# Transposing the attention probabilities in two halves of 64 rows, each into a PSUM bank of its own

## The chip, the cores and the metric

One core of a Trainium2 chip runs the whole program. The metric is device time in microseconds (us), as a median of several runs. Five engines work side by side, each through its own list of instructions: PE (TensorE, matmuls; its weight loads are listed apart as PEld), DVE (VectorE), ACT (ScalarE), POOL (GpSimd) and SP (SyncE, which issues most transfers). They wait for each other by semaphores.

## The reference, cut to what matters

```
# attention: B, H, S, D = 8, 8, 576, 64, a causal window of 64 positions
scores = scale * np.matmul(q, k.transpose(0, 1, 3, 2))
mask = (rel >= 0) & (rel < window)            # rel = query position - key position
scores = np.where(mask, scores, -1000000000.0)
attn = np.exp(scores - scores.max(-1))        # divided by its sum + 1e-9
attn_out = np.matmul(attn, v)
# x = attn_out as 4608 tokens of 512 = 8 heads x 64
# experts: a token with x @ w_skip > 0 goes to the best of 8 experts by x @ w_gate
# out = x + gate_w * (relu(x @ w1[e]) @ w2[e]) for those tokens, out = x for the others
```

## The kernel before, in words

**Tiles.** The 4608 tokens are worked off in 36 tiles `t` of 128 queries: two blocks of 64 queries (`hf` = 0 and 1), all 8 heads. By its window a block of queries sees its own 64 keys and the 64 before them, so the scores of a tile are 128 queries x 8 heads x 128 keys.

**The steps of one tile.** `score(t)` (L238, L252): the mask (`band`) and then the products of q and k go into the PSUM tile `ps`, two banks, on quarters of PE's array (64 rows x 64 columns each). `soften(t)`: DVE takes the maximum (L271) and subtracts it (L272), ACT makes the exponential (L277); the result `s` lies in SBUF with the 128 queries on the partitions. `transpose_p(t)` (L279 to L287): PE turns `s` head by head, so that the keys lie on the partitions, into `pt` in PSUM, and ACT copies that to `ptm` in SBUF (L286). `tile_out(t)` with `av_tile` (L388): PE multiplies `ptm` by the values (and by ones for the sums, and by columns for the router) into `av`; DVE reads it from L399 on and divides by the sums. A transpose on PE loads the data as weights and streams an identity matrix through them.

**The gate.** In most tiles a piece of the router's projection of v goes through PE as well: `pw` (L336) or its transpose `pk` (L344). ACT copies both out of PSUM. `pt`, `pw` and `pk` share one pair of PSUM banks (tag "t", bufs=2) in turn.

**The order.** It is written out by hand. Iteration t issues `score(t + 1)`, the gates, `soften(t)`, `tile_out(t - 2)`, `transpose_p(t - 1)`, and between these the loads, the stores and the routing of finished groups of 6 or 8 tiles: counts on PE (L517, L520), lists of tokens on POOL and PE (L560). Each engine keeps to its order. So PE goes scores, gate, `av`, transposes, and ACT goes gate copy, exponential, copies of `pt`.

After the attention part comes the expert part, whose work starts from the routed lists; its matmuls keep PE busy to nearly the end. The short transposes `px` (L895) that the prediction reads belong to it: token rows turned before an expert's first product, some with only 32 rows.

Of the kernel before, what the change touches and what calls it, by code (L numbers as in the profile page):

```python
# [8 lines left out]
F32 = mybir.dt.float32  # L9
# [11 lines left out]
P = 128  # L21
# [123 lines left out]
def window_attention_moe(ctx: ExitStack, tc, a, out):  # L145
    nc = tc.nc
# [6 lines left out]
    psum = ctx.enter_context(tc.tile_pool(name="psum", bufs=1, space=PSUM))  # L153
# [9 lines left out]
    ident = const.tile([P, P], F32, name="ident")  # L163
# [115 lines left out]
    def transpose_p(t):  # L279
        s = ss.pop(t)  # L280
        ptm = ptp.tile([P, 8, P], F32, name="ptm")
        for r in range(2):
            pt = psum.tile([P, 4, P], F32, name="pt", tag="t", bufs=2)
            for p in range(4):
                nc.tensor.transpose(pt[:, p], s[:, 4 * r + p], ident)  # L285
            nc.scalar.copy(ptm[:, 4 * r : 4 * r + 4], pt)  # L286
        pts[t] = ptm  # L287

    ss, pts, vs = {}, {}, {}
# [847 lines left out]
    with tc.manual_schedule():  # L1137
# [42 lines left out]
        for t in range(NT - 1):  # L1180
            m, r = divmod(t, 9)
# [18 lines left out]
            if t >= 1:  # L1200
                transpose_p(t - 1)
# [22 lines left out]
        drip()  # L1224
        routes(1)
        transpose_p(NT - 2)
        raise_e(NT - 1)
        routes(1)
        drip()
        tile_out(NT - 2, psc.tile([P, 2, 4, P], F32, name="ps").rearrange("p a b c -> p a (b c)"))  # L1230
        drip()
        routes(1)
        transpose_p(NT - 1)
        pxs = [psc.tile([P, 2, 4, P], F32, name="ps"), pav.tile([P, 2, 512], F32, name="av")]
        pxs = [pxs[0][:, 0].rearrange("p a b -> p (a b)"), pxs[1][:, 0]]
# [173 lines left out]
    with tc.If(more > 0):  # L1409
        with tc.For_i(0, more, 1) as i:  # L1410
# [15 lines left out]
            for qi in range(NQ):  # L1426
                both = []
# [58 lines left out]
```

## Time and profile before

| | |
|---|---|
| time, median of 3 runs | 415.93 us (414.9 to 416.22) |
| the profiled execution's own time | 417.13 us |
| its span in the profile | 415.4 us |
| granted TensorE clock, mean | 0.995 |
| transposes in the attention part | 288, on record with 282 ns each |
| copies of them on ACT | 72, 581 ns each |

The span is the profiled execution from its first to its last instruction; its time is a little longer. Instructions on PE overlap, so that the time on record of one is longer than the distance to the next: what a stage costs is read from its piece in the chain.

### The profile page before, as it was taken

To read this page: it belongs to the slowest core of one execution; us is meant where nothing else is said; L and a number is where in the kernel's file an instruction comes from. 1 tells how busy PE (TensorE), PEld (TensorE's weight loads), DVE (VectorE), ACT (ScalarE), POOL (GpSimd) and SP (SyncE) were. 2 spreads that over 40 slices of the span, in tenths; PEclk is the share of its full clock that TensorE was granted. 3 is DMA by queue.
4 is the path that set the end of the run, shared out by engine and by line. 5 is a ranking of instruction groups with operands and counts; after the bars stand their busy time and mean duration, and the time that the engine had idled before them with its cause. 6 is when DMAs were issued, how large, how long until landed. Compare 5 with 4: busy or idle time off the path is not lost.

```text
span 415.4 us, 11519 instructions
## 1 busy us (share of the span) xinstructions
PE 392.6 (95%) x4623; PEld 327.6 (79%) x4623; DVE 301.7 (73%) x547; ACT 216.7 (52%) x373; POOL 159.6 (38%) x296
## 2 busy tenths in 40 slices
PE   8898999999999898989999999999999999999794
PEld 3576787877878677879988798898898889988673
DVE  3586899899799795999468789565455486658871
ACT  2675877767677694536224445244335345533450
POOL 1521268567958878477204114022024030100110
PEclk9999999999999998999999999999999999999999
DMA  8999999999995694866605777645136886741510
GB/s 279 408 336 386 405 361 377 411 395 300 394 412 186 212 358 145 234 230 194 224 0 175 255 271 216 225 170 174 55 134 208 266 259 211 245 157 52 184 48 21
DMA packets 35096, 99.41 MB, mean 239 GB/s; under 512 B 4480, under 2 KB 5888, under 8 KB 35040
## 3 DMA queue, kind: packets, MB, share of 16 engines
q1 hardware_dynamic: 30560, 87.22, 60.1%
q0 software_dynamic: 3200, 9.58, 6.5%
q10 hardware_dynamic: 1280, 1.85, 1.2%
q8 instruction: 37, 0.61, 0.6%
q14 instruction: 19, 0.16, 0.1%
HBM read 84.57 MB, written 14.39 MB: 238 GB/s over the span
## 4 chain that ended last, share of the span: by engine, by line
PE 64%; issue 13%; DMA 10%; DVE 4%; POOL 4%; ACT 3%; POOLq 0%; ACTq 0%; SPq 0%; another core or an unknown queue 0%; DVEq 0%
PE av L388 8%; PE pt L285 7%; PE p L918 6%; PE ps L252 5%; PE p L919 5%; PE p L920 5%; DMA out<-yo,les 5%; PE yv L918 3%; PE yv L919 3%; PE yv L920 3%; PE ps L238 2%; PE pw L336 2%; PE yw L919 2%; PE yw L918 2%; PE yw L920 2%
## 5 line engine op out<-in xcount | busy, mean ns | idle before, releaser
L852 DVE TENSOR_TENSOR wlo<-raw,whi 128x1024 fp32r<-128x1024 f32 x70 | 86.3, 1244 | 15.9 <-ACT whi L848 14.2
L1022 POOL DMA_INDIRECT out<-yo,les x18 | 17.6, 976 | 147.7 <-DVE yo L1013 138.0
L982 ACT ACTIVATE hh<-p 128x256 fp32r<-128x256 f32 (+4 forms) x56 | 22.9, 410 | 98.3 <-PE p L920 84.5
L848 ACT CAST whi<-raw 128x1024 fp32r<-128x1024 f32 x72 | 74.2, 1046 | 0.0
L918 PE MATMUL p<-xp,whi 128*128 128x256 f32 (+4 forms) x192 | 58.2, 303 | 0.4 <-ACT xp L896 0.4
L919 PE MATMUL p<-xp,whi 128*128 128x256 f32 (+4 forms) x192 | 57.1, 297 | 0.2 <-DVE xp L899 0.2
L920 PE MATMUL p<-xp,wlo 128*128 128x256 f32 (+4 forms) x192 | 56.8, 296 | 0.0
L985 DVE SCALAR_TENSOR_TENSOR hl<-p,hh 128x256 fp32r<-128x256 f32 (+4 forms) x56 | 25.2, 451 | 43.5 <-ACT hh L982 28.0
L277 ACT ACTIVATE s<-s 128x1024 f32<-128x1024 f32 x36 | 38.1, 1059 | 31.8 <-DVE s L272 31.7
L271 DVE TENSOR_REDUCE mx<-ps 128x8 f32<-128x1024 f32 x36 | 43.6, 1211 | 6.7 <-PE ps L252 6.7
L272 DVE TENSOR_TENSOR s<-ps,mx 128x1024 f32<-128x1024 f32 x36 | 44.1, 1225 | 4.6
L388 PEld LDWEIGHTS av<-vm,ptm 128*64 128x64 f32 x992 | 34.7, 136 | 13.3 <-issue 6.2
L388 PE MATMUL av<-vm,ptm 128*64 128x74 f32 x992 | 39.8, 230 | 4.2 <-issue 1.7
L286 ACT COPY ptm<-pt 128x512 f32<-128x512 f32 x72 | 38.2, 581 | 8.2 <-PE pt L285 8.0
L285 PE MATMUL pt<-ident,s 128*128 128x128 f32 x288 | 39.9, 282 | 0.0
L918 PEld LDWEIGHTS p<-xp,whi 128*128 128x128 f32 x192 | 36.2, 188 | 3.0 <-ACT xp L896 0.7
L919 PEld LDWEIGHTS p<-xp,whi 128*128 128x128 f32 x192 | 36.2, 188 | 1.2 <-DVE xp L899 0.5
L920 PEld LDWEIGHTS p<-xp,wlo 128*128 128x128 f32 x192 | 36.1, 188 | 0.0
L252 PE MATMUL ps<-k,q 64*64 64x128 f32 x1024 | 33.6, 270 | 1.5 <-DMA q<-qT 1.5
L285 PEld LDWEIGHTS pt<-ident,s 128*128 128x128 f32 x288 | 31.6, 143 | 2.5 <-issue 0.3
L252 PEld LDWEIGHTS ps<-k,q 64*64 64x64 f32 x1024 | 30.0, 133 | 4.3 <-issue 2.3
L357 POOL COPY vm<-vm 64x1184 f32<-64x1184 f32 x16 | 18.6, 1166 | 31.9 <-ACT vm L356 26.7
(243 smaller groups left out, 819.4 us busy)
## 6 DMA issues: line engine op xcount, KB each, us to landing
raw<-wq SPq DMA_DIRECT2D x72, 512.0 KB
vm<-vp SPq DMA_DIRECT2D x15, 592.0 KB
vT<-vT SPq DMA_DIRECT2D x16, 512.0 KB
out<-x SPq DMA_DIRECT2D x32, 256.0 KB
q<-qT SPq DMA_DIRECT2D x14, 512.0 KB
k<-kT SPq DMA_DIRECT2D x7, 640.0 KB
k<-kT SPq DMA_DIRECT2D x7, 512.0 KB
kt<-kT SPq DMA_DIRECT2D x8, 256.0 KB
```

The lines of the kernel that those rows point to most:

```text
L252: nc.tensor.matmul(ps[64 * hf : 64 * hf + 64, r, p], q[h, p], k[h, :, p], start=False, stop=p == 3, skip_group_check=True,)
L271: nc.vector.tensor_reduce(mx, flat, axis=AX.X, op=ALU.max)
L272: pace[0] = nc.vector.tensor_tensor(s, flat, mx.unsqueeze(2).to_broadcast([P, 8, P]), op=ALU.subtract)
L277: nc.scalar.activation(s, s, AF.Exp, scale=0.125)
L285: nc.tensor.transpose(pt[:, p], s[:, 4 * r + p], ident)
L286: nc.scalar.copy(ptm[:, 4 * r : 4 * r + 4], pt)
L388: nc.tensor.matmul(av[64 * hf : 64 * hf + 64, h // 4, (h % 4) * VW : (h % 4 + 1) * VW], ptm[:, (h % 2) * 4 + h // 2, 64 * hf : 64 * hf + 6 ...
L848: nc.scalar.copy(ring[n % RING][0], raw_of[n])
L852: by.tensor_tensor(lo, raw_of[n], hi.bitcast(F32), op=ALU.subtract)
L918: nc.tensor.matmul(o, lh, rh, start=first, stop=False, skip_group_check=parts)
L919: nc.tensor.matmul(o, lh, rl, start=False, stop=False, skip_group_check=parts)
L920: nc.tensor.matmul(o, ll, rh, start=False, stop=last, skip_group_check=parts)
```

## The change

`transpose_p` splits the 128 queries of a tile into the halves 0 to 63 and 64 to 127. Each half has one PSUM bank that holds its 64 queries for all 8 heads; before, each bank held all 128 queries for 4 heads. The sixteen transposes alternate between the halves, and each reads 64 partitions of `s` and the matching 64x64 corner of the identity. The two copies come after all of them, and each writes eight runs of 64 columns into `ptm`, where the layout is as before.

```
-        for r in range(2):
-            pt = psum.tile([P, 4, P], F32, name="pt", tag="t", bufs=2)
-            for p in range(4):
-                nc.tensor.transpose(pt[:, p], s[:, 4 * r + p], ident)
-            nc.scalar.copy(ptm[:, 4 * r : 4 * r + 4], pt)
+        both = [psum.tile([P, 8, 64], F32, name="pt", tag="t", bufs=2) for _ in range(2)]
+        halves = [slice(64 * hf, 64 * hf + 64) for hf in range(2)]
+        for h in range(8):
+            for pt, q in zip(both, halves):
+                nc.tensor.transpose(pt[:, h], s[q, h], ident[q, q])
+        for pt, q in zip(both, halves):
+            nc.scalar.copy(ptm[:, :, q], pt)
```

On PE, a tile in the middle of the attention part, from the gate to the next tile's mask, before the change (`pt_916` and `pt_922` are the two banks; "waits" names the engine whose semaphore is waited for; x13 means 13 such rows):

```order
L336 MATMUL pw_875<-vT_701,wg_77 32x256 x3
L388 MATMUL av_888<-vm_312,ptm_835 64x74 [waits DVE_49]
L388 MATMUL av_888<-vm_312,ptm_835 64x74
L388 MATMUL av_888<-vm_312,ptm_835 64x74 [waits Activation_49]
L388 MATMUL av_888<-vm_312,ptm_835 64x74 x13
L285 MATMUL pt_916<-ident_74,s_806 128x128 [waits PE_49]
L285 MATMUL pt_916<-ident_74,s_806 128x128 x3
L285 MATMUL pt_922<-ident_74,s_806 128x128 [waits Activation_49]
L285 MATMUL pt_922<-ident_74,s_806 128x128 x3
L238 LDWEIGHTS identb_75
```

The same place of such a tile with the change (two lines further down in the program; the pattern of the last two rows of transposes goes on to sixteen):

```order
L338 MATMUL pw_774<-vT_571,wg_77 32x256 x3
L390 MATMUL av_787<-vm_210,ptm_727 64x74 [waits DVE_49]
L390 MATMUL av_787<-vm_210,ptm_727 64x74 [waits Activation_49]
L390 MATMUL av_787<-vm_210,ptm_727 64x74 x14
L286 MATMUL pt_811<-ident_74,s_698 128x64 [waits PE_49]
L286 MATMUL pt_812<-ident_74,s_698 128x64 [waits Activation_49]
L286 MATMUL pt_811<-ident_74,s_698 128x64
L286 MATMUL pt_812<-ident_74,s_698 128x64
```

The wait for ACT, which frees the second bank, has moved from the fifth transpose to the second, and in `av` the wait for the second copy from the third matmul to the second. On ACT, the gate's copy, the exponential and the copies of `pt` in one tile before the change:

```order
L338 COPY vw_731<-pw 128x256 [waits PE_49]
L277 ACTIVATE s<-s 128x1024 [waits DVE_49]
L286 COPY ptm<-pt 128x512 [waits PE_49] x2
L364 COPY vm<-vm 64x592
L377 COPY vt<-vm 64x592
```

and with it:

```order
L340 COPY vw_779<-pw 128x256 [waits PE_49]
L277 ACTIVATE s<-s 128x1024 [waits DVE_49]
L288 COPY ptm<-pt 128x8x64 [waits PE_49] x2
L366 COPY vm<-vm 64x592
L379 COPY vt<-vm 64x592
```

Nothing changes place here; the two copies have another target shape.

## Rows read from the trace of the kernel before

**Rows 1.** The page: busy us (share of the span) xinstructions of each engine.

```profile
PE 392.6 (95%) x4623; PEld 327.6 (79%) x4623; DVE 301.7 (73%) x547; ACT 216.7 (52%) x373; POOL 159.6 (38%) x296
```

**Rows 2.** Busy time of each engine in a stretch, PE's clock, DMA share, GB/s.

```profile
core 0: us, PE busy (x) PEld busy (x) DVE busy (x) ACT busy (x) POOL busy (x), PEclk, DMA share, GB/s
34.99:90.67 55.68, 55.63 (x1165) 44.73 (x1161) 50.52 (x94) 41.34 (x74) 29.34 (x59) 1.00 1.03 392
```

**Rows 3.** The chain that ended last, 36 to 48 us: start, us, what.

```profile
37.67 1.02 PE pt L285 x8
38.70 0.34 PE ps L238 x4
39.03 0.87 PE ps L252 x32
39.91 0.57 PE pw L336 x8
40.48 1.18 PE av L388 x32
...
43.90 0.37 PE pk L344 x2
```

**Rows 4.** The same chain, 78 to 95 us.

```profile
77.99 0.22 PE pt L285 x2
```

**Rows 5.** DVE in order of time: start, us, instruction [idle before <-releaser].

```profile
34.99 1.22 DVE L271 TENSOR_REDUCE mx<-ps 128x8 f32<-128x1024 f32 x1
...
41.71 0.17 DVE L399 TENSOR_SCALAR r<-av 128x8 f32<-128x8 f32 x1 [0.23 <-PE av L388]
...
90.67 1.21 DVE L271 TENSOR_REDUCE mx<-ps 128x8 f32<-128x1024 f32 x1
...
124.24 1.21 DVE L271 TENSOR_REDUCE mx<-ps 128x8 f32<-128x1024 f32 x1
...
127.90 1.21 DVE L271 TENSOR_REDUCE mx<-ps 128x8 f32<-128x1024 f32 x1
```

**Rows 6.** DVE's waits from 24 to 95 us: total us, times, longest.

```profile
DVE r L399 <- PE av L388: 4.2, 6, 3.1
DVE r L399 <- PE av L560: 0.7, 1, 0.7
DVE r L399 <- PE av L520: 0.6, 2, 0.4
```

**Rows 7.** Weight loads in order of time: four short transposes; scores after a stall.

```profile
287.29 0.32 PEld L895 LDWEIGHTS px<-ident,xg 32*128 32x128 f32 x4 [0.20 <-issue]
...
16.31 0.13 PEld L252 LDWEIGHTS ps<-k,q 64*64 64x64 f32 x1 [1.36 <-issue]
...
16.31 0.18 PEld L252 LDWEIGHTS ps<-k,q 64*64 64x64 f32 x4 [1.36 <-issue]
```

**Rows 8.** ACT, one tile in order of time; then its groups by shape.

```profile
37.60 1.06 ACT L277 ACTIVATE s<-s 128x1024 f32<-128x1024 f32 x1 [0.42 <-DVE s L272]
38.69 1.07 ACT L286 COPY ptm<-pt 128x512 f32<-128x512 f32 x2
...
L286 ACT COPY ptm<-pt 128x512 f32<-128x512 f32 x72 | 38.2, 581 | 8.2 <-PE pt L285 8.0
L356 ACT COPY vm<-pk 128x144 f32<-128x144 f32 x16 | 4.5, 284 | 5.1 <-PE pk L344 3.4 <-POOL lh L468 0.8 <-DMA vm<-vp 0.6
```

**Rows 9.** In order of time: waits between DVE, POOL and PE after 95 us.

```profile
95.10 0.30 POOL L537 TENSOR_TENSOR gds<-gds,gohb 128x64 f32<-128x64 f32 x1 [2.01 <-DVE gds L530]
...
112.41 0.20 DVE L482 TENSOR_REDUCE gmx<-lg 128x6 f32<-128x48 f32 x1 [1.94 <-POOL lg L469]
...
138.44 1.25 PE L388 MATMUL av<-vm,ptm 128*64 128x74 f32 x32 [1.43 <-POOL vm L357]
```

**Rows 10.** ACT in order of time: a copy that waits for PE.

```profile
140.69 0.58 ACT L286 COPY ptm<-pt 128x512 f32<-128x512 f32 x1 [1.59 <-PE pt L285]
```

**Rows 11.** The waits over the whole span: the scores for q.

```profile
PE ps L252 <- DMA q<-qT: 1.5, 2, 1.1
```

## The prediction

> **What bounds the kernel now.** Read the busy shares first [rows 1]: TensorE (PE) 95%, VectorE (DVE) 73%. That is an average over an attention part (36 tiles, to about 165 us) and an expert part; the change touches the first alone. So the next view is the chain that ended last, in order of time [rows 3]: from 36 to 48 us, as in most of 34 to 113 us, nothing but PE stands in it, piece after piece. One tile is band 0.34, scores 0.87, a gate piece (`pw` 0.57 in some tiles, `pk` 0.37 in others), `av` 1.18 and the transposes `pt` 1.02. With `pw` that is 3.98 us, with `pk` 3.78.
>
> A chain shows what ended last and not how close the next engine is, so DVE comes next. Where DVE waits for nobody, it starts a tile's maximum 3.66 us after the one before (124.24 to 127.90 [rows 5]). Between 34.99 and 90.67 us it starts 14 further tiles in 55.68 us, 3.98 each. It waits at L399, the first instruction that reads `av` [rows 5, 6]. DVE is therefore only 0.1 to 0.3 us a tile behind PE, and this small number, not the 1.02 us of the transposes, is what the change can win.
>
> DMA is as full as it gets in this stretch (share 1.03, 392 GB/s [rows 2]), but the scores wait for a load of q only twice in the whole span, 1.5 us in all [rows 11].
>
> **What the change costs and saves on PE.** Eight transposes of 128x128 become sixteen of 64x128 into 128x64, in pairs that use rows 0 to 63 and 64 to 127 of the array. Each streams 64 columns in place of 128 and loads as many weight columns as before, 128.
>
> Streaming: in the chain two old transposes take 0.22 us [rows 4], so 0.11 us for 128 columns. The scores are recorded as 32 matmuls of 128 columns on quarter tiles, and take 0.87 us [rows 3]: 0.109 for each four. Four tiles in the time of one means that tiles which share columns and differ in rows stream side by side. So a new pair streams in about 0.055 us.
>
> Loading: the four `px` transposes at 287.29 us have 32 rows, 128 weight columns and short matmuls, all in one row group; the four loads take 0.32 us; with one taken as long as the scores' load below, 0.13, that is (0.32 - 0.13)/3 = 0.063 us from load to load [rows 7]. That is the floor within one row group. Do the two groups load side by side? When the scores start after a stall, one load lasts 0.13 us on record and all four together 0.18 [rows 7]: the fourth begins 0.05 after the first, not the 0.18 that three loads of 0.06 in a row would make. The four tiles differ in rows and in columns, so this speaks for overlap between row groups without isolating it.
>
> So a pair costs between 0.06 (loads side by side) and 0.12 (in series). I take 0.0625, nearest to the rows that hold both facts. The old stage is 8 x 0.109 = 0.87 plus 0.15 around it = 1.02. The new one is 8 x 0.0625 = 0.50 plus 0.15 = 0.65. **Saved: 0.37 us of PE a tile**, 5.2 over the 14 tiles above.
>
> The same load, by the Trainium skill ("TensorE: Matmul & The Clock Gate", section "LDWEIGHTS (loading the stationary operand)"), takes columns/1.2 ns whatever the rows, which is about 107 ns for 128 columns, an estimate from that page. By that rule the pair would be bound by its load and the stage would stay at 1.0 us. The `px` row of this trace shows 0.06 us, so the measurement decides for the smaller price; the rule makes one of the rivals.
>
> **ScalarE (ACT).** Each copy moves 512 elements a row as before; only the target is now eight runs of 64. The copy of 512 takes 581 ns, and one of 144 elements in runs of nine 284 [rows 8], so short runs cost nothing that shows: I take 0, at most 0.05 each. The copies now wait for all sixteen transposes, where the first waited for four. In a steady tile this is hidden: the copies of 38.69 us stand in ACT's order behind the exponential of 37.60 to 38.66 [rows 8]; the transposes of that tile stand in the chain from 37.67 [rows 3], and the shorter stage would be done by 38.3. Without that cover (ACT waits for PE, as at 140.69 [rows 10]) the first copy starts at the eighth pair, not the fourth transpose: 0.50 against 0.44, plus the start of a stage, 0.1 us later. There are some five such tiles; I count -0.3 us.
>
> The second transpose now needs the second bank at once, half a stage earlier. Queued behind it on PE is the next tile's score, which DVE reads a whole tile later. The bank's reader is the gate's copy, which ACT makes before the exponential, so I count nothing; if it came late it would cost up to 0.4 in that tile.
>
> **What of it reaches the end.** In 34.99 to 90.67 PE's 55.63 us busy [rows 2] would need 50.4, less than DVE's 14 x 3.66 = 51.2. DVE becomes the bound, and what is won is what DVE waited. From below: the waits listed for 24 to 95 us are 4.2 + 0.7 + 0.6 = 5.5, less the one of 3.1, a single stall that I take to have another cause, so 2.4; shorter waits aren't listed [rows 6]. From above: 55.68 - 51.2 = 4.4, too much, as DVE has routing work of its own in these tiles. I take 3.5, a little over the middle, since a wait of under 0.2 stands in nearly every tile.
>
> After 95 us little more is won. GpSimd (POOL) starts a stretch at 95.10, released by DVE, and works through it until DVE waits 1.94 for it at 112.41; at 138.44 PE waits 1.43 for it again [rows 9]. These are shifted with DVE's 95 us, and a tile won between is lost there. The expert part follows attention and shifts as a whole.
>
> Sum: -3.5 + 0.3 = **-3.2 us**. The profiled execution took 417.13 us (span 415.4), 1.2 above the median of 415.93, so 413.9 beside it and **412.7** as a median. A difference under 0.3% (1.25 us) can't be told from none.
>
> **Rivals.**
> 1. *The pairs load in series* (the other side). Place: the transposes. 16 x 0.0625 + 0.15 = 1.15 us, 0.13 more than now. In the 14 or so tiles before 95 us in which DVE waits, that is 1.8 us, and PE's tiles after 112 us (3.78 and 3.98 against DVE's 3.66) lose a few tenths more: +2.0, 417.9 us. It decides from a pair of 0.109 us upward. For it: no row has two loads that differ in rows alone. Against: four loads within 0.05 us.
> 2. *A load costs what its columns cost at half the rate*, 0.107 us, in both groups at once. The stage stays at 1.0 and the time at 416. Against it the `px` row; for it only that full transposes at 0.11 would hide such a load.
> 3. *PE gets faster and something else takes the wait.* After DVE's subtraction come the exponential, the copies, then the gate, `av` and L399. In the tile of 37.60 us [rows 3, 8] the first copy ends at 38.69 + 0.54 = 39.23; 0.15 for a change of stage, 0.57 of gate, 1.18 of `av` and the 0.05 from its end to L399 make 41.2, against DVE free at 41.71 - 0.23 = 41.5 [rows 5]. There are only 0.3 us of room: if the copies slip by that, or the DMA at 392 GB/s can't deliver faster, less than 1.25 us is left: about 415.3.
>
> **Chances.** The forecast 0.64, rival 1 0.14, rival 2 0.10, rival 3 0.12. So faster 0.64, same 0.22, slower 0.14. The range: the upper bound of DVE's waits, 4.4 + 0.5 for the tiles from 24 us, and 1 us for a shorter chain in the last tiles make about -6, 409.9. Upward it takes in rivals 2 and 3 and reaches toward rival 1: 417.0. The forecast's own range is 410 to 414.6.
>
> **What would show it.** The transposes' piece of the chain at about 0.65 us and a new pair every 0.06; the loads 16 to a tile. DVE's starts 3.66 to 3.75 apart between 35 and 91 us, with L399's waits nearly gone; POOL's wait at 112 still there, slightly longer. ACT's copies still at 0.58. Wrong at the first step if the stage is 1.0 or more; wrong at the second if it is 0.65 and DVE's starts stay at 3.9 with the wait for ACT or a load in the chain.

## The result and the profile after

The changed kernel takes 420.01 us (median of 4 runs, 419.56 to 421.99) beside 416.0 of the old one on the same chip: 1.0108 times, with a 95% interval of 1.0082 to 1.0134. **It is slower by 4.0 us; forecast was 3.2 faster.** The profiled execution took 419.56 us, with a span of 417.7.

The first part of the change did what was forecast. The page's rows for the engines and for the copies (busy, mean ns of one | idle before):

```profile
PE 387.5 (93%) x4911; PEld 323.2 (77%) x4911; DVE 302.2 (72%) x547; ACT 217.4 (52%) x373; POOL 158.9 (38%) x296
...
L288 ACT COPY ptm<-pt 128x512 f32<-128x512 f32 x72 | 38.3, 583 | 8.7 <-PE pt L286 8.5
```

The copies last 583 ns, as before, and PE is busy 5 us less [rows 1]. The chain that ended last, as in [rows 3], shows the shorter stage and what came with it:

```profile
40.30 1.19 PE av L390 x32
41.48 0.64 PE pt L286 x16
42.13 0.34 PE ps L238 x4
42.47 0.65 PE ps L252 x21
43.12 0.94 issue
44.05 0.65 PE ps L252 x11
44.70 0.37 PE pk L346 x2
```

The stage takes 0.64 us (forecast 0.65). But in the middle of the scores, after 21 of 32 matmuls, PE stands still for 0.94 us and waits for nothing that the profile shows ("issue"). The same stretch of DVE's tiles as in [rows 2], now 13 tiles in place of 14:

```profile
core 0: us, PE busy (x) PEld busy (x) DVE busy (x) ACT busy (x) POOL busy (x), PEclk, DMA share, GB/s
34.60:90.70 56.10, 49.90 (x1195) 39.36 (x1191) 46.71 (x86) 39.87 (x70) 26.72 (x53) 1.00 1.02 386
```

A tile takes 56.10 / 13 = 4.32 us, where it took 3.98. At 34.60 the changed kernel was 0.4 us ahead; at its last maximum (156.66 us in place of 152.90) it is 3.8 behind, which is the loss. PE's waits from 24 to 95 us (total, times, longest), where the old kernel had one "issue" wait, of 1.7 us:

```profile
PE av L390 <- issue: 3.1, 4, 1.5
PE ps L252 <- issue: 2.0, 2, 1.0
PE pt L286 <- issue: 1.1, 2, 0.9
PE pw L338 <- issue: 0.6, 1, 0.6
PE pw L338 <- DMA vT<-vT: 0.5, 1, 0.5
```

Nine waits of 6.8 us name no one ("issue"), and 0.5 us is a wait for a load. They strike the scores, `av`, the transposes and the gate alike, so it is not one instruction's fault. PE in order of time shows their rhythm:

```profile
44.05 0.65 PE L252 MATMUL ps<-k,q 64*64 64x128 f32 x11 [0.94 <-issue]
44.63 0.44 PE L346 MATMUL pk<-ident,vw 128*128 128x128 f32 x2
45.00 1.26 PE L390 MATMUL av<-vm,ptm 128*64 128x74 f32 x32
46.19 0.71 PE L286 MATMUL pt<-ident,s 64*128 64x64 f32 x16
46.83 0.41 PE L238 MATMUL ps<-band,identb 64*64 64x512 bf16 x4
47.07 1.04 PE L252 MATMUL ps<-k,q 64*64 64x128 f32 x32
48.04 0.64 PE L338 MATMUL pw<-vT,wg 128*32 128x256 f32 x8
48.61 0.99 PE L390 MATMUL av<-vm,ptm 128*64 128x74 f32 x22
50.07 0.60 PE L390 MATMUL av<-vm,ptm 128*64 128x74 f32 x10 [0.47 <-issue]
...
54.89 0.60 PE L252 MATMUL ps<-k,q 64*64 64x128 f32 x11
56.53 0.88 PE L252 MATMUL ps<-k,q 64*64 64x128 f32 x21 [1.04 <-issue]
...
61.32 0.60 PE L390 MATMUL av<-vm,ptm 128*64 128x74 f32 x11
63.45 0.87 PE L390 MATMUL av<-vm,ptm 128*64 128x74 f32 x21 [1.53 <-issue]
```

From 44.05 to the next stall stand 11 + 2 + 32 + 16 + 4 + 32 + 8 + 22 = 127 matmuls, in the next stretch 127 again, then 126. (An fp32 matmul of the program is recorded as two passes, so sixteen for the scores are 32.) Each has its weight load, so a stall comes every 254 instructions or so. With PE's few semaphore instructions counted as well, in the order in which the records start, it is 256 to the instruction: eight of the nine stalls stand at record 193 or at 193 plus a multiple of 256. The ninth (0.5 us at 27.41) does not, and its cause stays open. What comes in such pieces is on the page, in the rows of queue 8 (packets, MB, share); first the changed kernel:

```profile
q8 instruction: 39, 0.64, 0.6%
```

and the old one:

```profile
q8 instruction: 37, 0.61, 0.6%
```

9822 PE instructions (4911 matmuls and as many loads) in 39 packets are 252 a packet; in the old kernel 9246 in 37 are 250, and a packet is 16 KB. With the semaphore instructions PE has 9945 records and 9359, and in every kernel of this case the number of packets in queue 8 is the number of PE's records divided by 256, rounded up. So PE's own instructions come through the DMA queues in blocks of 256. The single records of the trace give both ends, in us from the span's start (every 256th PE instruction counted from one stall, beside the packets of queue 8):

```
kernel   a block begun   packet of the next starts, ends   next block begun   stall
after         44.05             47.68   48.57                  50.07           0.47
after         50.07             54.12   55.02                  56.53           1.04
after         56.53             60.73   62.04                  63.45           1.53
before        52.35             55.03   56.03                  58.66           none
before        58.66             61.04   62.05                  64.30           none
after        136.35            136.64  137.79                 144.00           none
```

In these rows of the changed kernel PE goes on 1.4 to 1.5 us after the packet's end (1.2 in the shortest of the eight stalls): that is the step from landing to execution. The packet starts 3.6 to 4.2 us after the block before it was begun where DMA is full, and 0.3 us after at 136 us, where it isn't. Together a block that ends in a stall takes about 6 us, and PE gets no more than 256 instructions in that time. The old kernel was close to it: 1165 matmuls and their loads in 55.68 us [rows 2] are 9.1 blocks, 6.12 us each, and its packets mostly ended 2.2 to 2.6 us before they were needed, about 1 us earlier than the 1.2 to 1.5 that PE needs. The changed kernel has 2 x 1195 / 13 = 184 instructions a tile in place of 2 x 1165 / 14 = 166. At the 6.01 us that its own blocks took in this stretch they make its 4.32 us a tile. That is a sum and no test, as both come from the same stretch; the tests are the kernels below with other counts.

The 3.6 to 4.2 us are not a fixed price of full queues. Between 33 and 95 us, at the same DMA share of 1.03, the old kernel's packets started 1.8 to 3.1 us after the block before was begun, and in the changed kernel blocks without a stall had theirs after 2.8 to 3.0 us and took 5.2 to 5.5 (begun at 69.49, 80.71 and 86.23). Why they started sooner is not shown.

### The profile page after: what moved, and what is told of

The parts are those of the page before. It is cut to its first block, busy times and chain, and to the rows that moved or that the text cites. A ratio compares the mean times of both kernels' runs of the same rounds, so it can differ in the third digit from the quotient of the medians.

```text
span 417.7 us, 12105 instructions
## 1 busy us (share of the span) xinstructions
PE 387.5 (93%) x4911; PEld 323.2 (77%) x4911; DVE 302.2 (72%) x547; ACT 217.4 (52%) x373; POOL 158.9 (38%) x296
## 4 chain that ended last, share of the span: by engine, by line
PE 42%; issue 21%; DMA 12%; DVE 12%; POOL 8%; ACT 3%; POOLq 0%; ACTq 0%; SPq 0%; DVEq 0%
PE av L390 6%; DMA out<-yo,les 5%; PE p L920 4%; PE p L921 4%; PE p L922 4%; PE ps L252 3%; DVE s L272 3%; PE pt L286 2%; DVE mx L271 2%; DMA q<-qT 2%; PE yv L920 2%; PE yv L921 2%; PE yv L922 2%; DVE x L403 2%; DMA raw<-wq 2%
## 5 line engine op out<-in xcount | busy, mean ns | idle before, releaser
L854 DVE TENSOR_TENSOR wlo<-raw,whi 128x1024 fp32r<-128x1024 f32 x70 | 85.0, 1226 | 15.8 <-ACT whi L850 15.6
L390 PEld LDWEIGHTS av<-vm,ptm 128*64 128x64 f32 x992 | 36.6, 139 | 16.7 <-issue 8.4
L390 PE MATMUL av<-vm,ptm 128*64 128x74 f32 x992 | 42.3, 234 | 7.2 <-issue 3.2
L252 PE MATMUL ps<-k,q 64*64 64x128 f32 x1024 | 35.2, 270 | 4.5 <-DMA q<-qT 2.4
L286 PE MATMUL pt<-ident,s 64*128 64x64 f32 x576 | 26.5, 231 | 1.1 <-issue 1.1
L734 POOL DMA_INDIRECT xg<-out,les x18 | 24.5, 1363 | 6.1 <-issue 4.6
```

Source lines behind the costliest of these rows:

```text
L252: nc.tensor.matmul(ps[64 * hf : 64 * hf + 64, r, p], q[h, p], k[h, :, p], start=False, stop=p == 3, skip_group_check=True,)
L286: nc.tensor.transpose(pt[:, h], s[q, h], ident[q, q])
L390: nc.tensor.matmul(av[64 * hf : 64 * hf + 64, h // 4, (h % 4) * VW : (h % 4 + 1) * VW], ptm[:, (h % 2) * 4 + h // 2, 64 * hf : 64 * hf + 6 ...
L854: by.tensor_tensor(lo, raw_of[n], hi.bitcast(F32), op=ALU.subtract)
```

## Experiments

Theory **F**: PE waits for blocks of its own instructions. Rivals: **D**, the loads of q, k and v can't come faster; **C**, the later copies; **P**, PE's own time decides; **G**, a block takes 6 us whatever else the queues carry; **H**, loads in pieces come late themselves. Behind each time stands its ratio to the old kernel on the same chip, with the 95% interval.

**1. Order of the halves, copies alone.** `half_by_half` keeps sixteen transposes but runs one half after the other; `late_copies` keeps the eight old transposes and copies after all of them.

```
half_by_half:  for pt, q in zip(both, halves):
                   for h in range(8):
                       nc.tensor.transpose(pt[:, h], s[q, h], ident[q, q])
late_copies:   for r, pt in enumerate(both): (four transposes of 128 rows)
               for r, pt in enumerate(both): nc.scalar.copy(...)
```

> The sixteen transposes in another order: all eight of one half of the queries, then all eight of the other, so that no two neighbours use different rows. As many PE instructions as the changed kernel, but a stage as long as the old one or longer. Theory F (PE waits for its own instructions, which come in blocks of 256 through the full DMA queues): the stage goes back to 1.0 to 1.2 us, the number of instructions decides all the same, the stalls without a named cause stay about 127 matmuls apart between 37 and 91 us, DVE's tiles stay at 4.2 to 4.4 us, 419 to 423 us. Rival D (the loads of q, k and v can't come faster than 373 GB/s): PE asks for them as slowly as before, so 416 to 418 us. Rival C (the copies that start after all sixteen): as D, 416 to 418, by the longer stage alone.

Measured 421.53 us, 1.0133 (1.0097 to 1.0168). The chain of `half_by_half`:

```profile
48.03 0.95 PE pt L286 x16
48.98 0.34 PE ps L238 x4
49.32 0.87 PE ps L252 x32
50.20 0.57 PE pw L338 x8
50.77 0.92 PE av L390 x22
51.68 0.15 issue
```

The stage is 0.95 us, still 0.07 less than the old 1.02, and yet the kernel is 1.3 per cent slower: neither PE's time nor a faster demand for loads can do that. Its 13 tiles from 36.23 to 93.47 us have the same 1195 matmuls, 4.40 us a tile, and nine of its ten unnamed stalls up to 100 us stand at record 193 plus a multiple of 256 again. F holds; D, C and P miss their times here.

> The old kernel with its eight transposes of 128 rows, but with both copies after all eight: the one part of the change that puts the copies later, with neither halves nor more instructions. Theory F: 416 to 416.5 us, tiles of 3.98 us between 35 and 91 us. Rival C: 418 or more, with ACT's copies in the chain.

Measured 416.48 us, 1.0014 (0.9991 to 1.0036): the copies cost next to nothing. C falls again.

**2. More instructions, at little PE time.** `pad_after` adds to the changed kernel eight matmuls of one column a tile, ahead of `av`:

```
for i in range(8):
    nc.tensor.matmul(av[64 * (i % 2) : 64 * (i % 2) + 64, 0, 4 * VW + i : 4 * VW + i + 1],
                     onesb[:, 0:64], onesb[:, 0:1], start=True, stop=True, ...)
```

> The changed kernel with eight more small matmuls a tile ahead of av (one column each, written where nobody reads): 16 more PE instructions a tile, as many as the change itself added, and little PE time, 0.1 to 0.25 us beside the 0.37 that the change took away. Theory F: the number of instructions decides: a tile of about 199 records at 256 in 6.0 us takes 4.6 to 4.7 us, 14 tiles 4 to 5 us more than in the changed kernel, 424 to 428 us, with stalls still 126 or 127 matmuls apart. Rival P (PE's own time decides): a tile stays shorter than the old one, 421 us or less.

Measured 426.8 us, 1.0292 (1.024 to 1.0343). In order of time the eight push `av` back by 0.15 us where nothing stalls:

```profile
52.00 0.29 PE L389 MATMUL av<-onesb 128*64 128x1 bf16 x8
52.15 1.23 PE L395 MATMUL av<-vm,ptm 128*64 128x74 f32 x32
```

The tiles from the seventh maximum to the twentieth, busy time and counts:

```profile
36.68:95.18 58.50, 51.18 (x1301) 40.70 (x1296) 46.95 (x87) 39.82 (x70) 26.65 (x53) 1.00 0.98 359
```

So PE's tile (3.61 with `pw` in the forecast, plus 0.15) is shorter than the old 3.98, and the kernel is 2.9 per cent slower than the old one. 2602 instructions in 58.50 us are 5.76 us a block. The page's queue 8 has 42 packets. Its stalls up to 95 us stand at record 193 plus a multiple of 256 as well, which here are mostly other instructions of the program than in the changed kernel; so do the two waits of 1.1 and 1.2 us that the list of waits puts down to DVE and ACT. P falls; with the place of the stalls, this is the run that carries the cause.

**3. Between old and new.** `every_other` has halves in odd tiles alone (`if t % 2:`), `bands2_after` two mask matmuls in place of four in 28 tiles, `late24` halves from tile 24 on (`if t >= 24:`).

> Halves in every other tile, the old transposes in the rest: a mean tile of some 175 PE instructions (old 167, changed 183) and a mean PE time of 3.8 us. Theory F: 175 at 256 in 6.0 us is 4.10 us a tile where the queues are full, 0.12 more than in the old kernel over some 14 tiles: 417 to 419 us, between the two, with stalls a block apart. Rival P (PE's own time): 414 to 415 us.

Measured 419.76 us, 1.0089 (1.0056 to 1.0121). On F's side, but above its range: half of the added instructions cost nearly as much as all. 1159 matmuls in the 13 tiles from 36.73 to 90.82 us are 178 instructions and 4.16 us a tile, 5.97 us a block.

> The changed kernel with two matmuls in place of four for the mask in the 28 tiles whose two blocks have the same mask (a doubled identity, 64 rows by 128 columns): four PE instructions fewer in such a tile, PE's time the same. Theory F: 2 per cent fewer instructions, 0.08 to 0.1 us a tile over some 16 tiles: 418 to 419.5 us. Rival P: 420 as before.

Measured 422.17 us, 1.0152 (1.0115 to 1.0189): a miss. The stretch has 2 per cent fewer instructions, but its blocks took 6.16 us in place of 6.01. So small a saving drowns in the spread of the blocks, 5.2 to 6.9 us in one execution.

> The halves in the last twelve tiles alone, where the queues are less full; the tiles before as in the old kernel. Theory F: no stall comes back, and PE's 0.37 us a tile count only where nothing else bounds: 413.5 to 416 us. If the halves hurt by themselves (copies, banks, switching the array): 417 us or more.

Measured 416.77 us, 1.0005 (0.9978 to 1.0033): above F's range and below what the rival named, and no different from the old kernel. PE's waits list no unnamed stall up to 170 us, as F said. Halves cost nothing clear of noise in those tiles, and win nothing either. That DVE and POOL bound them would explain this, but no run tests it.

**4. Are the full queues to blame?** First by less traffic. `after_less_v` and `before_less_v` leave out loads (`if n < NVB:` ahead of the load of vp, else the buffer of group n - 4).

> The changed kernel without the loads of v for the third to the eighth sequence: the buffers keep older values of v, so x and what follows from it are not the reference's; gates, routing and all work on the engines stay. The loads fall by 592 KB per group of four blocks, about a fifth of the traffic there. Theory F: the blocks of instructions come sooner, the stalls go from about 55 us on, DVE's tiles fall from 4.3 toward 3.7, and the kernel is 2 to 5 us faster than the old kernel with the same loads left out. Rival D: it gains as well, so this run doesn't tell F from D. Rival C: it stays 3 to 5 us slower than the old kernel with the same loads left out.

> The old kernel without the same loads of v (x and what follows is not the reference's). Theory F: its stretch from 35 to 91 us is bound by PE's work, 3.98 us a tile, which needs no load sooner: 415 to 416.5 us. Rival D, if the loads bound the old kernel too: 413 or less.

Measured 420.96 us, 1.0102 (1.0068 to 1.0136), and 416.03 us, 1.0009 (0.9987 to 1.0031). The old kernel was not bound by its loads, which speaks against D. But the changed one got no faster: a miss for F as I had put it. The DMA share from 60 to 95 us fell to 0.82 only as a mean; where PE stalled there it was still 0.98 to 1.03 while the block was awaited.

Then by loads in pieces, so that fewer bytes lie ahead: by rows (`split2_after`, `split2_before`, `split4_after`: `k[z, ...]` for z of 64 or 32 rows), and by columns (`splitf_after`, `splitf_before`).

> The changed kernel with each load of q, k, vT and vp from the third group on cut into two of 64 rows each: the same bytes, but since about eight loads are under way at a time, half as many bytes lie in the queues ahead of a block of PE's instructions. Theory F (the block waits behind the loads): loads land in 4 to 5 us where they took 7 to 9, the blocks come about 1.5 us sooner, the stalls without a named cause between 37 and 91 us (7.5 us in all in the changed kernel) fall below 3, and the time to 412 to 416 us. Rival G (a block of instructions takes its 6 us whatever else is under way): the stalls stay, 419 to 422 us. Rival H: more issues on SP delay the loads themselves, PE waits for q and vT, 421 us or more.

> The old kernel with the same loads cut in two. Theory F: it has one stall of that kind, 1.7 us, so little to win: 414.5 to 416.5 us. Rival H: 418 us or more.

> The changed kernel with the same loads cut into four of 32 rows each. Theory F: loads land in 2 to 4 us, the stalls go altogether, DVE's tiles at 3.7 to 3.8 us between 35 and 91 us, 411 to 415 us unless SP, at about 0.4 us an issue and 20 issues a group of 2.25 tiles, comes late. Rival G: 419 to 422 us. Rival H: 422 us or more.

> The changed kernel with the loads of q, k, vT and vp from the third group on cut in two along their columns, all 128 rows in each piece (the cut by rows moved 266 GB/s in place of 373). Theory F: if the pieces move at the full rate, half as many bytes lie ahead of a block of instructions: it comes after 4 to 5 us in place of 6, the stalls fall below 3 us, 412 to 416 us. Rival G (a block takes 6 us whatever is under way): 419 to 421 us. Rival H (pieces of half the size move more slowly, as by rows): the loads are late, 425 us or more.

> The old kernel with the same cut along the columns. Theory F: 414.5 to 416.5 us. Rival H: 420 us or more.

Measured: 450.46 us, 1.078 (1.0724 to 1.0837); 448.33, 1.0764 (1.0713 to 1.0815); 464.87, 1.1156 (1.1117 to 1.1196); 419.04, 1.007 (1.0042 to 1.0099); 417.44, 1.0029 (1.0008 to 1.0051). A load of 64 rows lands about as late as one of 128; `split2_after` from 24 to 95 us:

```profile
DMA packets 7962, 18.92 MB, mean 266 GB/s; under 512 B 1305, under 2 KB 1817, under 8 KB 7948
```

against 373 GB/s in the changed kernel, with the queues as full: rival H, and no test of F. (By PE's waits the changed kernel's unnamed stalls between 37 and 91 us are 5.7 us, not the 7.5 of the expectation.)

By columns the rate held better (342 GB/s), and a load of q landed in 5.6 us in place of 8.9. The times miss F's 412 to 416, and the 414.5 to 416.5 of the old kernel too. But the halves cost 419.04 - 417.44 = 1.6 us with loads cut so, where they cost 4.0 without, so part of the loss may have gone, which would speak for F; 419.04 lies in G's range as well. The trace can't decide it. Its execution was the slowest of nine (422.29 us); there the queues stayed at 0.99 to 1.01, and in blocks that ended in a stall the next packet started 2.5 to 4.3 us after the block was begun. So whether the bytes under way set the delay stays open.

Last by more traffic in a stretch that had room. `twice_after` and `twice_before` issue the loads of q and vT twice from group 12 on.

> The changed kernel with the loads of q and vT of the last four groups issued twice (same data, same place), 4 MB more between about 102 and 140 us, where the queues are busy to 0.7 to 0.98 in the changed kernel. Theory F (a block waits behind the loads): in that stretch the blocks come 3.5 to 4.5 us after the one before was begun, where several came after 0.3 to 2.5; stalls a block apart up to 140 us, 2 to 5 us slower than the changed kernel: 422 to 425 us. Rival G (a block's 6 us don't depend on what is under way): no new stalls without a named cause; only loads that come late, with their names, if anything, 420 to 421.

> The old kernel with the same loads issued twice. Theory F: it uses a block in 6.2 us where PE doesn't wait, so the blocks come just in time: at most one or two stalls under 1 us, 416 to 418 us. If the loads themselves come too late for q or vT, both kernels lose alike, by waits that name the load.

Measured 448.07 us, 1.0754 (1.0716 to 1.0793), and 443.57, 1.0648 (1.0602 to 1.0694). The second load waits for the first (SP waits 19.5 us for q and 16.2 for vT), the loads come late under their own name (the gate waits 23.1 us for vT in four waits), and nothing is learnt of F or G. So traffic that no one waits for:

```
+ spare = dram.tile([10, P, 4, 4, 64], F32, name="spare")
+ if 24 <= t < 34:
+     nc.sync.dma_start(spare[t - 24], a["qT"][t % 8, :, 0:4])
```

> The changed kernel with ten copies of 512 KB from memory to memory, which nobody reads, one in each of the tiles 24 to 33, about 112 to 150 us, where the queues are busy to 0.72 to 0.88 in the changed kernel. Theory F (a block waits behind the other traffic): the blocks begun there come after 6 us or more, stalls without a named cause there rise from 2 us or so to 4 to 8, 422 to 426 us. Rival G (a block takes its time whatever is under way): no more such stalls than in the changed kernel; 420 to 421 us, unless loads come late with their names.

> The old kernel with the same copies. Theory F: it takes 256 instructions in about 6 us there, so it loses less than the changed kernel does, 416 to 419 us. Rival G: 416 to 417 us.

Measured 425.1 us, 1.0244 (1.0215 to 1.0272), and 417.48 us, 1.0052 (1.0025 to 1.0079). The stretch of 112 to 157 us, busy times, clock, DMA share and GB/s, of the changed kernel,

```profile
112.00:157.00 45.00, 39.62 (x932) 31.36 (x928) 38.12 (x75) 31.82 (x55) 35.05 (x94) 1.00 0.79 281
```

and of `spare_after`:

```profile
112.00:157.00 45.00, 40.26 (x959) 31.73 (x955) 37.08 (x71) 31.51 (x57) 34.81 (x89) 1.00 0.97 355
```

PE's waits in that stretch, the changed kernel's

```profile
PE ps L238 <- issue: 0.6, 1, 0.6
...
PE av L390 <- issue: 0.2, 1, 0.2
```

and those of `spare_after`:

```profile
PE av L391 <- issue: 2.2, 2, 1.6
PE ps L253 <- issue: 1.2, 2, 0.7
...
PE ps L239 <- issue: 0.6, 1, 0.6
```

The waits that name no one rise from 0.8 to 4.0 us, and no load is waited for. In the records, the blocks begun at 116.55, 123.04, 129.22 and 135.29 us had their successor's packet start 3.7 to 4.5 us later and took 6.1 to 7.0 us; the one begun at 142.26, where the DMA share had dropped to 0.18, 1.1 us later. In the changed kernel the same four blocks, begun at 113.72, 120.01, 125.89 and 131.07, had theirs 4.0, 3.5, 2.1 and 0.4 us later. G falls: here a block comes later because the queues are fuller. `spare_before` has no wait of this kind in the stretch; it is 1.7 us slower than the old kernel, and I cannot name the place. With the copies in both kernels the halves cost 425.1 - 417.48 = 7.6 us, where they cost 4.0 without: 3.6 more, near the 3.2 by which the unnamed waits rise.

No version tried beats the old kernel.

## Why the prediction was wrong

- **The stage, 0.65 us:** right (0.64), by the mechanism named: the loads of the two row groups lie side by side. (0.64 - 0.15) / 8 is 0.061 us a pair, 0.0625 forecast. Rivals 1 and 2 fall with it. Half by half, (0.95 - 0.15) / 16 gives 0.05 us from load to load within one row group. So two in series would take 0.10, and a pair takes 0.061; but the 0.063 that the prediction called the floor within one row group is no floor, and that the pair came out so near to it is in part luck. Even in series sixteen would not have cost more than eight old transposes.
- **The copies, no cost:** right (583 ns, and `late_copies`). The 0.3 us for later copies can't be told from none.
- **"DVE becomes the bound, and what is won is what DVE waited":** the step that failed. With PE's work at 3.4 to 3.6 us a tile the next bound was at first not DVE at 3.66 but the supply of PE's own instructions, a cost that the prediction's sum does not have: 4.32 us a tile over the stretch. DVE's waits at L401 rose instead: 5.6 + 1.6 + 0.3 = 7.5 us from 24 to 95 us, against 5.5 [rows 6]. The same thirteen tiles took 51.89 us in the old kernel (34.99 to 86.88) and 56.10 now: 4.2 more, less the 0.4 by which the first of them was ahead, is the 3.8 found at the last maximum. Of the 4.2 us, 3.6 are lost by the maximum at 66.31 (63.13 in the old kernel); from 40 to 73 us the chain holds PE's pieces and stalls alone. Later DVE does become the bound in part: from 73 to 113 us more than half of the chain is DVE and ACT, as in the rows below, where the old kernel's holds PE alone, and only 0.6 is lost up to 90.70 and nothing after. So the forecast's order of engines held in part there; the stalls before had already cost the 3.6 us. The chain of the changed kernel from 73.63 us:

```profile
73.63 0.69 DVE x L403
74.32 0.19 DVE lh L409
74.51 1.09 DVE mx L271
...
75.72 1.24 DVE s L272
...
76.98 1.06 ACT s L277
...
78.06 0.59 ACT ptm L288
```

- **What I could have read:** I counted matmuls by their time and never by their number. Rows 2 hold it: 256 instructions in 6.12 us. At DVE's pace the new tile of 184 asks for 256 in 3.66 x 256/184 = 5.1 us, while DMA stands at 1.03. The old kernel's one stall of 1.7 us without a cause stands behind the 3.1 us of DVE's wait that I set aside (DVE goes on at 33.81); it came at such a boundary (33.49 us in the records, 1.3 us after a packet's end). That a block could not come in 5.1 us, the old trace alone does not say.
- **After 95 us:** right in kind. POOL's wait and the expert part shift with what is behind them; nothing of the loss is recovered before the last maximum, and in the profiled executions the spans differ by 2.3 us at the end.
- **Rival 3** named DMA as what might take the wait, but as late loads, with 415.3 us; the loads were waited for 0.5 us. What DMA delivered late was PE's instructions.

The Trainium skill ("Runtime: NRT & Kernel Launch", section "Instruction fetch mechanics") says that an engine's instructions come in blocks of 256 through a DMA queue of its own, and that crossing into the next block is mostly hidden. The first part agrees with the stalls 256 records apart and the 16 KB packets of queue 8 here. The second does not hold in the changed kernel's stretch: at a DMA share of 1.0 a crossing cost up to 1.5 us.

## What to carry to other kernels

Before splitting matmuls into more and shorter ones, divide a stretch's PE instructions (each matmul and each load, as the trace records them) by 256 and compare the time of a block with 6 us where DMA is full. In the stalled stretches of the kernels above a block took 5.8 to 6.2 us in the mean, whatever its instructions were. At 6.0 us an instruction costs about 23 ns, so the old transpose of 0.109 us cost 47 ns of supply and its pair of halves, 0.061 us of PE, 94. Stalls that name no one, at equal counts of instructions, point to this; count between two of them before looking for a slow operand. A kernel whose PE is busy all the time can be near this limit without a stall in the stretch to show for it, as the old one was with 55.63 of 55.68 us busy.

## What the runs showed of the hardware

- A block of 256 PE instructions took 5.2 to 6.9 us in the changed kernel's stalled stretch. In blocks begun after 37 us that ended in a stall of 0.4 us or more, the packet of the next started 3.4 to 4.5 us after the block was begun, in `after` and `spare_after` at a DMA share near 1; where the changed kernel's share was under 0.6, 0.1 to 0.4 us after. From the packet's end to the first instruction of a block that PE had stalled for it was never below 1.2 us. How the engines choose between packets stays open.
- Stalls of this kind stand 256 PE records apart, or a multiple of it, in all kernels traced that have them, and the packets of queue 8 number PE's records over 256, rounded up (37 to 42).
- A load cut into halves of 64 rows moves 266 GB/s where whole loads move 373; cut along the columns 342.
